# Splitting batch 0's state operands in high and low parts from the fifth step on

## The chip, the cores and the metric

One core of a Trainium2 chip runs the whole program. The metric is the device time of one execution in microseconds (us); of several runs the median is given. [...]

## What is computed

Three stages follow each other. `x` has 8 batches of 8 heads, 512 rows and 64 columns, and `state` has 32 rows for each head.

```
scores  = x @ state.T / 8          a  = softmax(scores)     xread = a  @ state
scores2 = state @ x.T / 8          a2 = softmax(scores2)    sread = a2 @ x
X   = concat(xread, sread) over rows, heads side by side     (4352 x 512)
X1  = (silu(X @ w_gate) * (X @ w_val)) @ w_out               (512 -> 1536 -> 512)
out = (h * sigmoid(1.702 h)) @ w2_out,  h = X1 @ w2_in       (512 -> 2048 -> 512)
```

All is fp32. The change is in the second line block, in `X @ w_gate` and `X @ w_val` of batch 0.

## The kernel before

**Weights through the state.** `xread` is never formed. Since `X @ w = a @ (state @ w)`, the kernel multiplies the states with the weights first. One such product, `sw[b, u, g]`, belongs to a batch b, a pair u of steps and a group g of four heads: 128 rows (four heads by 32 states) by 512 columns. `quad_job` (L615) makes them for four batches at a time: two matmuls (L628) of 64 contraction rows, two copies out of PSUM into a tile `qs` (L634 on ScalarE, L635 on VectorE), and a store of the rows of the other batches to DRAM through ScalarE's DMA queue (`move`, L651). Batch 0's own rows go from `qs` straight into the operand tile by SyncE's queue (L647), for u from `OWN` = 2 on. For u below 2, `state_weights` makes batch 0's operand directly.

**Two kinds of product.** Matmuls on plain fp32 operands (`mm_whole`, L336) stand in the trace as two MATMUL records each. The other way splits each operand in a high part that is rounded to the type fp32r and the low part that is left over, and takes three passes: high by high, low by high, high by low (`mm_rows`, L329 to L331). `mm_state` (L710) makes the products of a step with the states' weights: batch 0 takes the plain way, all others the split one.

**Steps.** A block of 512 rows (a batch) takes F1 = 12 steps f of 128 columns. A step has a gate product, work of its places 0, a value product, work of place 1, the output product of the step before (12 matmuls of three passes, L951 to L953), and work of place 2. Steps 2u and 2u + 1 use `sw[b, u, g]`. ScalarE takes Silu of the gate product (L976), VectorE multiplies (L991), then the result is split for the output product: high part on ScalarE (L796), low part on VectorE, or on GpSimd in batch 0 (L797).

**What else batch 0 carries.** While batch 0's steps run (about 25 to 160 us), all weights arrive and are put together from two halves of their bits, `whole_slot`: L202 and L203 on ScalarE, L211 and L212 on VectorE, L215 on GpSimd; the weights of `w_out` are split too (L249, L250). The attention of batch 1 is done beside it (table `BLOCK0`): scores (copied by L461), maximum (L488, L492), exponentials (L502, L507, each with a load of ScalarE's function table before and after), sums, transposes (L539).

**Order.** The program is recorded in the order in which it is written, each engine keeps its own order of instructions, and so do the DMA queues. `plan_weights` puts work at (step, place), here by `job_places` for `quad_job`. For later batches it puts `fetch` (a DMA from DRAM into a tile `xf` of which there are two, on ScalarE's queue, L660) one step ahead of `cut_fetched` (L666 on ScalarE, L667 on GpSimd), which splits that tile into an operand `xo`. Batch 1's fetches for u = 0 stand at step 9 of batch 0.

Of the kernel before, what the change touches and what calls it, by code (L numbers as in the profile page):

```python
# [8 lines left out]
F32 = mybir.dt.float32  # L9
# [3 lines left out]
ALU = mybir.AluOpType  # L13
# [60 lines left out]
def kernel(  # L74
# [25 lines left out]
    NS = state.shape[2]  # L100
    DM = H * D
    FF1 = w_gate.shape[1]
    FF2 = w2_in.shape[1]
    P = 128
    KD = DM // P
    F1 = FF1 // P
    U1 = F1 // 2
# [7 lines left out]
    v, a, pe, pool_e, sy = nc.vector, nc.scalar, nc.tensor, nc.gpsimd, nc.sync  # L115
# [4 lines left out]
    work = ctx.enter_context(tc.tile_pool(name="work", bufs=2))  # L120
    xp = ctx.enter_context(tc.tile_pool(name="xop", bufs=1))
# [13 lines left out]
    def f32(t):  # L135
        return t.bitcast(F32)
# [147 lines left out]
    def need_whole(key):  # L284
        while pos["done"] <= where[key]:
            before = pos["done"], pos["begun"]
            whole_slot()
            assert before != (pos["done"], pos["begun"]), key
# [37 lines left out]
    def mm_rows(ps, pairs):  # L326

        for k, (wh, wl, xh, xl) in enumerate(pairs):
            pe.matmul(ps, wh, xh, start=k == 0, stop=False)  # L329
            pe.matmul(ps, wl, xh, start=False, stop=False)  # L330
            pe.matmul(ps, wh, xl, start=False, stop=k == len(pairs) - 1)  # L331

    def mm_whole(ps, pairs):

        for k, (w, x_) in enumerate(pairs):
            pe.matmul(ps, w, x_, start=k == 0, stop=k == len(pairs) - 1)  # L336
# [14 lines left out]
    def at():  # L351
        if extra:
            extra.append(extra.pop(0))
            if extra[0] != "at":
                return psa.tile([P, 512], F32, name="at", tag=extra[0])
        return pst.tile([P, 512], F32, name="at", tag="at")
# [246 lines left out]
    sw = {}  # L603
# [13 lines left out]
    OWN = 2  # L617

    def quad_job(qd, u, k, late=False):


        if qd == 0:
            need_whole(("gv", u, k))
        w = whole[u * KD + k]
        ps = [at(), at()]
        for hl in range(2):
            r = slice(hl * 64, hl * 64 + 64)
            pe.matmul(ps[hl], quad_t[qd][r, k], w[r], start=True, stop=True)  # L628
        pos["jobs"] += 1
        if qd == 0 and not late or pos["jobs"] % 3 == 0:  # L630
            t = ap.tile([P, 2, DM], F32, name="qs", tag="qs", bufs=2)
        else:
            t = work.tile([P, 2, DM], F32, name="qs", tag="raw", bufs=RAWS)
        a.copy(t[:, 0], ps[0])  # L634
        v.tensor_copy(t[:, 1], ps[1])  # L635
        g, q = divmod(k, 2)
        skip = NS * (1 - qd)
        if q == 0:
            quads[qd, u, g] = dp.tile([4 * (P - skip), DM], F32, name=f"sw{qd}_{u}_{g}")
        rows = quads[qd, u, g].rearrange("(q h p) m -> q p h m", q=2, h=2)  # L640
        moved[qd].append((rows[q], t[skip:]))
        if qd == 0 and u >= OWN:
            if q == 0:
                sw[0, u, g] = x_tiles(xp, u % 2 * 2 + g, DM)
            for hl in range(2):
                r = slice(q * 64 + hl * NS, q * 64 + hl * NS + NS)
                sy.dma_start(f32(sw[0, u, g][0][r]), t[:NS, hl])  # L647

    def move():
        for to, t in moved.pop(0):  # L650
# [3 lines left out]
    fetched = {}  # L654
# [7 lines left out]
    def cut_fetched(b, u, g, home=None):  # L662
        t = fetched.pop((b, u, g))
        pl, tag = home or (xp, f"x{u % 2 * 2 + g}")
        x_ = pl.tile([P, 2, DM], F32R, name="xo", tag=tag)
        a.copy(x_[:, 0], t)  # L666
        pool_e.tensor_tensor(x_[:, 1], t, f32(x_[:, 0]), op=ALU.subtract)  # L667
        sw[b, u, g] = x_[:, 0], x_[:, 1]

    def job_places(b):  # L670

        if b == 0:
            own = [-2, 0, 1, 2]
            first = [(n, 0, k) for k, n in enumerate((0, 1, 2, 3))]
            last = [(n, 1, k) for k, n in enumerate((28, 30, 32, 34))]
            return [(n, 0, u, k) for n, u, k in first + last] + [
                (6 * (u - 1) + own[k], 0, u, k) for u in range(OWN, U1) for k in range(KD)
            ]
        if b < 4:
            return [(n, 1, *divmod(8 * (b - 1) + j, KD)) for j, n in enumerate((3, 6, 12, 15, 18, 24, 30, 33))]  # L680
        return []

    def plan_weights(plan, i):


        b = order1[i]
        nb = order1[i + 1] if i + 1 < NB1 else None
        if nb == B:
            nb = None

        def put(f, place, fn, *args):
            plan.setdefault((f, place), []).append(lambda: fn(*args))

        for n, qd, u, k in job_places(b):
            put(n // 3, n % 3, quad_job, qd, u, k, n >= 3 * F1 - 6)
        for g in range(2):
            if 0 < b < B:
                put(b == 1, g, cut_fetched, b, 1, g)
                if b == 1:
                    put(0, g + 1, fetch, b, 1, g)  # L700
                for u in range(2, U1):
                    put(2 * u - 3, g + 1, fetch, b, u, g)
                    put(2 * u - 2, g + 1, cut_fetched, b, u, g)
            if nb is not None:
                put(9, g, fetch, nb, 0, g)
                put(10, g, cut_fetched, nb, 0, g, (ae, f"a{g}") if b == B else None)
                if nb > 1:
                    put(11, g, fetch, nb, 1, g)

    def mm_state(ps, b, f, t):  # L710

        c = slice(t * 2 * P + f % 2 * P, t * 2 * P + f % 2 * P + P)
        pairs = []
        if b == 0:
            mm_whole(ps, [(f32(sw[b, f // 2, g][0])[:, c], f32(groups[b, g].a[:, 0])) for g in range(2)])
            return
        for g in range(2):
            wh, wl = sw[b, f // 2, g]
            at_ = groups[b, g].a
            pairs.append((wh[:, c], wl[:, c], at_[:, 0], at_[:, 1]))  # L720
        mm_rows(ps, pairs)
# [6 lines left out]
    groups = {}  # L728
# [70 lines left out]
    def x_tiles(pl, k, N):  # L799
        t = pl.tile([P, 2, S], F32R, name="xo", tag=f"x{k}")  # L800
        return t[:, 0, :N], t[:, 1, :N]
# [98 lines left out]
    for i, blk in enumerate(order1):  # L900
# [5 lines left out]
        if blk + 1 < B:  # L906
            plan_batch(plan, blk + 1)
        plan_weights(plan, i)
        if i == NB1 - 3:
            plan.setdefault((F1 - 2, 2), []).append(load_tail)  # L910
# [51 lines left out]
        def product(ps, f, t):  # L962
            if not tail:
                mm_state(ps, blk, f, t)
                return
            c = slice(t * 2 * P + f % 2 * P, t * 2 * P + f % 2 * P + P)
            w = [units["gv", f // 2, k] for k in range(KD)]
            mm_rows(ps[:, :N], [(w[k][:, 0, c], w[k][:, 1, c], *xop[k]) for k in range(KD)])
# [362 lines left out]
```

## Time and profile before

| what | value |
|---|---|
| median of 3 runs | 1504.39 us (1501.16 to 1505.3) |
| the profiled execution's own time | 1508.42 us |
| its span, first to last instruction | 1506.6 us |
| TensorE (PE) busy | 1475.1 us, 98% |
| VectorE (DVE) busy | 913.0 us, 61% |
| ScalarE (ACT) busy | 685.0 us, 45% |
| GpSimd (POOL) busy | 394.8 us, 26% |
| mean granted clock of TensorE | 0.992 |

The shares are means over the whole program. Batch 0 is about a tenth of it and has its own limits, so it has to be read by its stretches of time. Times in rows are us from the start of the span; where a row groups several records, the second number is the time from the first's start to the last's end. A matmul's own length includes what overlaps with the next one, so the cost of a matmul is the distance from one start to the next.

### The profile page before, as it was taken

The page shows a single profiled execution, that of the slowest core. Times are in us where ns is not written, and L with a number is a line of the kernel's source. Part 1 is how long each engine was busy: PE and PEld are TensorE (multiplying, and loading weights), DVE is VectorE, ACT ScalarE, POOL GpSimd, SP SyncE. Part 2 cuts the span into 40 slices and gives each one's busy share as a digit, 9 for nine tenths or more (in the row PEclk, how much of TensorE's full clock was granted, in tenths as well). Part 3 has the DMA queues.
Part 4 walks back from the last instruction along what each step waited for, and adds up shares of the span by engine and source line. Part 5 has one row for each costly group of instructions (what it writes and reads, how often), then busy time and mean ns, then how long its engine had stood idle before and what let it go on. Part 6 is the DMA issues. An engine that isn't in the chain of part 4 may idle for free.

```text
span 1506.6 us, 21223 instructions
## 1 busy us (share of the span) xinstructions
PE 1475.1 (98%) x7688; PEld 1197.5 (79%) x7688; DVE 913.0 (61%) x1600; ACT 685.0 (45%) x1247; POOL 394.8 (26%) x325
## 2 busy tenths in 40 slices
PE   7989999999999999999999999999999999999998
PEld 3445677777787777889788889999999999999997
DVE  6885565656679887953334335665655666656554
ACT  6766454545567666644454333233332333333222
POOL 2665322222234544556655421000000000000000
PEclk8999999999999999999999999999999999999999
DMA  7974333333455655422766656565565656564653
GB/s 212 293 239 144 123 109 116 114 110 109 134 183 168 193 178 179 138 85 82 234 233 248 232 184 209 187 222 171 193 215 185 221 180 238 168 238 159 214 183 130
DMA packets 138480, 269.30 MB, mean 179 GB/s; under 512 B 46728, under 2 KB 57992, under 8 KB 138376
## 3 DMA queue, kind: packets, MB, share of 16 engines
q1 hardware_dynamic: 114680, 223.64, 45.4%
q10 hardware_dynamic: 23696, 44.31, 8.9%
q8 instruction: 61, 1.00, 0.3%
q14 instruction: 43, 0.35, 0.1%
HBM read 202.11 MB, written 63.70 MB: 176 GB/s over the span
## 4 chain that ended last, share of the span: by engine, by line
PE 56%; DMA 7%; DVE 3%; ACT 2%; issue 2%; POOL 1%; ACTq 0%; SPq 0%; POOLq 0%; DVEq 0%
PE acc L339 8%; PE acc L340 8%; PE acc L341 8%; DMA xf<-sw 5%; PE gv L1232 4%; PE gv L1231 4%; PE gv L1230 4%; PE at L1230 3%; PE at L1231 3%; PE at L1232 3%; PE gv L329 2%; PE gv L330 1%; PE gv L331 1%; PE acc L953 1%; PE gv L322 1%
## 5 line engine op out<-in xcount | busy, mean ns | idle before, releaser
L797 DVE TENSOR_TENSOR h<-sg,h 128x512 fp32r<-128x512 f32 (+1 forms) x240 | 191.6, 798 | 136.2 <-ACT h L796 134.3
L796 ACT CAST h<-sg 128x512 fp32r<-128x512 f32 (+1 forms) x251 | 149.8, 597 | 183.8 <-DVE sg L991 80.8
L339 PE MATMUL acc<-wo,h 128*128 128x512 f32 x512 | 200.6, 392 | 0.0
L340 PE MATMUL acc<-wo,h 128*128 128x512 f32 x512 | 200.6, 392 | 0.0
L341 PE MATMUL acc<-wo,h 128*128 128x512 f32 x512 | 199.2, 389 | 0.0
L667 POOL TENSOR_TENSOR xo<-xf,xo 128x512 fp32r<-128x512 f32 x84 | 112.4, 1341 | 240.5 <-ACT xo L666 234.2
L1254 ACT ACTIVATE sg<-wt 128x512 f32<-128x512 f32 x56 | 35.4, 632 | 299.9 <-DVE wt L1252 299.9
L951 PE MATMUL acc<-h,wu 128*128 128x512 f32 (+1 forms) x428 | 166.6, 389 | 0.0
L953 PE MATMUL acc<-h,wu 128*128 128x512 f32 (+1 forms) x428 | 163.9, 383 | 1.9 <-DVE h L797 1.9
L952 PE MATMUL acc<-h,wu 128*128 128x512 f32 (+1 forms) x428 | 163.6, 382 | 0.0
L329 PE MATMUL gv<-a,xo 128*128 128x512 f32 x336 | 139.6, 415 | 3.8 <-ACT sg L976 3.5
L330 PE MATMUL gv<-a,xo 128*128 128x512 f32 x336 | 134.2, 399 | 0.0
L331 PE MATMUL gv<-a,xo 128*128 128x512 f32 x336 | 133.6, 398 | 0.0
L991 DVE TENSOR_TENSOR sg<-gv,sg 128x512 f32<-128x512 f32 (+1 forms) x107 | 70.5, 659 | 89.5 <-PE gv L331 31.6
L341 PEld LDWEIGHTS acc<-wo,h 128*128 128x128 f32 x512 | 96.2, 188 | 20.9
L339 PEld LDWEIGHTS acc<-wo,h 128*128 128x128 f32 x512 | 96.6, 189 | 17.1
L340 PEld LDWEIGHTS acc<-wo,h 128*128 128x128 f32 x512 | 96.6, 189 | 15.8
L1252 DVE TENSOR_TENSOR wt<-wt,gv 128x256 f32<-128x256 f32 x56 | 23.6, 421 | 136.8 <-PE gv L1232 136.8
L951 PEld LDWEIGHTS acc<-h,wu 128*128 128x128 f32 x428 | 81.1, 189 | 24.0 <-issue 7.6
L953 PEld LDWEIGHTS acc<-h,wu 128*128 128x128 f32 x428 | 81.1, 189 | 19.9 <-DVE h L797 3.8
L1232 PE MATMUL gv<-xo,wu 128*128 128x256 f32 x336 | 95.4, 284 | 0.0
L1231 PE MATMUL gv<-xo,wu 128*128 128x256 f32 x336 | 95.1, 283 | 0.0
(178 smaller groups left out, 3407.2 us busy)
## 6 DMA issues: line engine op xcount, KB each, us to landing
wo<-w2b SPq DMA_DIRECT2D x128, 512.0 KB
wc<-w2c SPq DMA_DIRECT2D x84, 512.0 KB
xf<-sw ACTq DMA_DIRECT2D x84, 256.0 KB
raw<-in_moe_w_out_dram SPq DMA_DIRECT2D x28, 512.0 KB
sw<-qs ACTq DMA_DIRECT2D x24, 512.0 KB
sw<-qs ACTq DMA_DIRECT2D x24, 384.0 KB
xn<-in_x_dram SPq DMA_DIRECT2D x16, 512.0 KB
y<-ev SPq DMA_DIRECT2D x16, 512.0 KB
```

Of the source, the lines that this page charges most:

```text
L329: pe.matmul(ps, wh, xh, start=k == 0, stop=False)
L330: pe.matmul(ps, wl, xh, start=False, stop=False)
L339: pe.matmul(ps, lh, rh, start=first, stop=False)
L340: pe.matmul(ps, lh, rl, start=False, stop=False)
L341: pe.matmul(ps, ll, rh, start=False, stop=last)
L796: a.copy(h_, src)
L797: eng.tensor_tensor(l_, src, f32(h_), op=ALU.subtract)
L951: pe.matmul(ps, w[:, 0, c], h[:, 0, :N], start=f == 0, stop=False)
L952: pe.matmul(ps, w[:, 1, c], h[:, 0, :N], start=False, stop=False)
L953: pe.matmul(ps, w[:, 0, c], h[:, 1, :N], start=False, stop=f == F1 - 1)
L1231: pe.matmul(ps, w[:, 1, c], x_[:, 0, kt], start=False, stop=False)
L1232: pe.matmul(ps, w[:, 0, c], x_[:, 1, kt], start=False, stop=kt == 1)
```

## The change

From step 4 (u = 2) on, batch 0's products with the states' weights take the split way. For this its own rows no longer go into the operand tile but into a tile `xf`, and `cut_fetched` splits that at step 2u - 1, place g. The other operand, the attention weights `a` of batch 0 (one tile for each group), is split once, after the last plain product: `cut_own` copies it on VectorE, ScalarE writes the rounded high part into a new tile, and VectorE subtracts. It stands at step 3, place 1 for the first group and place 2 for the second.

```diff
         if qd == 0 and u >= OWN:
             if q == 0:
-                sw[0, u, g] = x_tiles(xp, u % 2 * 2 + g, DM)
+                fetched[0, u, g] = work.tile([P, DM], F32, name="xf", tag="xf", bufs=2)
             for hl in range(2):
                 r = slice(q * 64 + hl * NS, q * 64 + hl * NS + NS)
-                sy.dma_start(f32(sw[0, u, g][0][r]), t[:NS, hl])
+                sy.dma_start(fetched[0, u, g][r], t[:NS, hl])
...
+    def cut_own(g):
+        t = work.tile([P, DM], F32, name="wt", tag="wt", bufs=3)
+        v.tensor_copy(t, f32(groups[0, g].a[:, 0]))
+        groups[0, g].a = a_ = groups[0, g].a_tile()
+        a.copy(a_[:, 0], t)
+        v.tensor_tensor(a_[:, 1], t, f32(a_[:, 0]), op=ALU.subtract)
...
         for g in range(2):
+            if b == 0:
+                put(3, 1 + g, cut_own, g)
+                for u in range(OWN, U1):
+                    put(2 * u - 1, g, cut_fetched, b, u, g)
             if 0 < b < B:
...
         pairs = []
-        if b == 0:
+        if b == 0 and f // 2 < OWN:
             mm_whole(ps, [(f32(sw[b, f // 2, g][0])[:, c], f32(groups[b, g].a[:, 0])) for g in range(2)])
```

In the changed kernel the lines behind `cut_own` stand 11 lower: L796 becomes L807, L976 L987, L991 L1002.

On VectorE at steps 3 and 4 of batch 0, before the change, from one copy of `quad_job` to the next:

```order
L635 COPY qs<-at 128x512
L211 TENSOR_SCALAR wf<-wf 128x512
L212 SCALAR_TENSOR_TENSOR wf<-raw,wf 128x512
L499 TENSOR_TENSOR sp<-sp,sq 128x512
L211 TENSOR_SCALAR wf<-wf 128x512
L212 SCALAR_TENSOR_TENSOR wf<-raw,wf 128x512
L211 TENSOR_SCALAR wt<-wt 128x512
L212 SCALAR_TENSOR_TENSOR wt<-raw,wt 128x512
L635 COPY qs<-at 128x512
```

The same stretch with the change:

```order
L635 COPY qs<-at 128x512
L672 COPY wt<-a 128x512
L675 TENSOR_TENSOR a<-wt,a 128x512
L211 TENSOR_SCALAR wf<-wf 128x512
L212 SCALAR_TENSOR_TENSOR wf<-raw,wf 128x512
L499 TENSOR_TENSOR sp<-sp,sq 128x512
L672 COPY wt<-a 128x512
L675 TENSOR_TENSOR a<-wt,a 128x512
L211 TENSOR_SCALAR wf<-wf 128x512
L212 SCALAR_TENSOR_TENSOR wf<-raw,wf 128x512
L211 TENSOR_SCALAR wt<-wt 128x512
L212 SCALAR_TENSOR_TENSOR wt<-raw,wt 128x512
```

The two copies and the two subtractions of `cut_own` stand ahead of the weight work and of the next copy of `quad_job`; each subtraction reads what ScalarE writes between it and the copy.

On ScalarE at step 3, with the change, from the copy of `quad_job` to the second part of `cut_own`:

```order
L634 COPY qs<-at 128x512
L674 CAST a<-wt 128x512
L666 CAST xo<-xf 128x512
L807 CAST h<-sg 128x512
L249 CAST wu<-wt 128x512
L202 ACTIVATE wf<-raw 128x512
L203 ACTIVATE raw<-raw 128x512
L651 DMA sw_3_0_702<-qs 96x2x512
L502 ACT_TABLE_LOAD
L502 ACTIVATE sp<-sp 128x512
L507 ACTIVATE e_742,sm<-ST,sm 128x512
L674 CAST a<-wt 128x512
```

Before, L634 was followed at once by the cast of h, and neither L674 nor L666 stood here; the cast of the second group now comes behind the exponentials of batch 1 and their table load.

On ScalarE at step 9, with the change, with what each instruction waits for:

```order
L461 COPY ST<-at 128x512 [waits PE_49]
L666 CAST xo<-xf 128x512
L660 DMA xf<-sw_0_0_373 128x1x512 [waits Pool_49]
L249 CAST wu<-wt 128x512
L634 COPY qs<-at 128x512 [waits DMAHW6_49,DMAHW7_49,DMAHW0_49,PE_49]
L666 CAST xo<-xf 128x512 [waits DMAHW2_49,DMAHW1_49]
L660 DMA xf<-sw_0_1_440 128x1x512 [waits Pool_49]
L807 CAST h<-sg 128x512 [waits DVE_49]
```

Before, the two L666 were not there and the two L660 waited for nothing. Each L660 now waits until GpSimd has subtracted from the `xf` tile that it refills (L667), and ScalarE's later instructions stand behind it.

## Rows read from the trace of the kernel before

**Rows 1.** Busy time by stretch of batch 0: steps 3/4, 5, 6 to 8, 9 to 11.
```profile
core 0: us, PE busy (x) PEld busy (x) DVE busy (x) ACT busy (x) POOL busy (x), PEclk, DMA share, GB/s
71.00:91.00 20.00, 16.59 (x44) 8.51 (x44) 18.29 (x25) 13.97 (x23) 13.15 (x11) 0.83 0.79 248
91.00:105.00 14.00, 13.45 (x45) 7.17 (x44) 11.88 (x19) 10.08 (x18) 8.39 (x7) 1.00 0.82 249
105.00:131.00 26.00, 26.00 (x91) 12.83 (x90) 13.54 (x19) 14.42 (x27) 15.80 (x12) 1.00 0.64 193
131.00:160.00 29.00, 28.32 (x91) 14.66 (x92) 15.63 (x29) 14.99 (x25) 11.88 (x9) 1.00 0.41 113
```

**Rows 2.** Timeline, TensorE, step 4: start, length, engine, line, operation, idle before.
```profile
73.77 1.88 PE L336 MATMUL gv<-a,xo 128*128 128x512 f32 x4
75.58 1.13 PE L628 MATMUL at<-wf,qt 64*128 64x512 f32 x4
...
82.03 2.96 PE L628 MATMUL at<-wf,qt 64*128 64x512 f32 x4 [3.41 <-DVE qs L635]
84.92 0.80 PE L951 MATMUL acc<-h,wu 128*128 128x512 f32 x1
...
90.30 1.13 PE L628 MATMUL at<-wf,qt 64*128 64x512 f32 x4
91.36 1.98 PE L336 MATMUL gv<-a,xo 128*128 128x512 f32 x4
```

**Rows 3.** Stretch within step 4: PE busy, granted clock, DMA share, GB/s.
```profile
85.00:90.00 5.00, 5.00 (x12) 0.50 0.65 201
```

**Rows 4.** Timeline, TensorE, first split product of batch 1 (six passes from 160.42).
```profile
160.42 0.40 PE L329 MATMUL gv<-a,xo 128*128 128x512 f32 x1
...
161.83 0.39 PE L951 MATMUL acc<-h,wu 128*128 128x512 f32 x1
```

**Rows 5.** Timeline, VectorE, steps 3 and 4.
```profile
74.30 0.69 DVE L635 COPY qs<-at 128x512 f32<-128x512 f32 x1
...
76.41 0.68 DVE L499 TENSOR_TENSOR sp<-sp,sq 128x512 f32<-128x512 f32 x1
77.01 1.52 DVE L211 TENSOR_SCALAR wf<-wf 128x512 uint32<-128x512 uint32 x1
...
79.17 0.42 DVE L211 TENSOR_SCALAR wt<-wt 128x512 uint32<-128x512 uint32 x1
...
81.21 0.68 DVE L635 COPY qs<-at 128x512 f32<-128x512 f32 x1
...
87.91 0.68 DVE L635 COPY qs<-at 128x512 f32<-128x512 f32 x1
```

**Rows 6.** Timeline, ScalarE, step 3 into step 4.
```profile
72.19 0.62 ACT L796 CAST h<-sg 128x512 fp32r<-128x512 f32 x1 [0.59 <-DVE sg L991]
...
75.42 1.28 ACT L502 ACT_TABLE_LOAD   x1 [0.63 <-ACT raw L203]
...
78.27 0.19 ACT L507 ACTIVATION_READ_ACCUMULATOR e<-ST,sm 128x1 f32 x1
```

**Rows 7.** Lines L667 and L666, later batches: duration ns min/median/max.
```profile
L667 POOL TENSOR_TENSOR xo<-xf,xo x84: 1263/1294/1785, 145.9 to 765.4; 128x512 fp32r<-128x512 f32 x84
...
L666 ACT CAST xo<-xf x84: 603/621/638, 145.2 to 764.6; 128x512 fp32r<-128x512 f32 x84
```

**Rows 8.** Timeline, TensorE, step 6, its only wait between 91 and 150 us.
```profile
104.53 1.09 PE L628 MATMUL at<-wf,qt 64*128 64x512 f32 x2 [0.55 <-DVE srd L574]
```

**Rows 9.** Timelines, steps 9 and 10: ScalarE, VectorE, TensorE.
```profile
134.57 0.58 ACT L461 COPY ST<-at 128x512 f32<-128x512 f32 x1 [1.12 <-PE at L336]
...
137.92 0.62 ACT L796 CAST h<-sg 128x512 fp32r<-128x512 f32 x1
...
142.30 0.69 DVE L510 TENSOR_REDUCE sq<-sp 128x16 f32<-128x512 f32 x1 [0.72 <-ACT sp L502]
...
144.12 0.69 DVE L635 COPY qs<-at 128x512 f32<-128x512 f32 x1
...
144.96 0.63 PE L539 MATMUL at<-ident,e 128*128 128x128 f32 x4
```

## The prediction

> **What bounds the kernel now.** I first read the busy time by stretch. TensorE is busy 98% of the span, but in batch 0 that is not so everywhere: at steps 3 and 4 it worked 16.59 of 20 us while VectorE worked 18.29, and at step 5 VectorE worked 11.88 of 14 us; from step 6 on VectorE is half idle and TensorE almost never [rows 1]. So there are two regimes: up to about 105 us VectorE's queue decides, behind that TensorE does.
>
> The timeline shows what this means. TensorE reaches a pair of `quad_job` matmuls in step 4 and waits 3.41 us for VectorE's copy of `quad_job` [rows 2], which starts at 81.21 [rows 5]. [...] Then VectorE's rows: one weight operation takes 0.42 us alone and 1.52 us at 77.01 [rows 5], where it stands beside work of GpSimd. Last I read what ScalarE does at steps 3 and 9, since the change puts new work ahead of things that others wait for.
>
> **The change part by part.**
>
> *Products.* A plain product of two groups takes 75.58 - 73.77 = 1.81 us [rows 2], a split one 161.83 - 160.42 = 1.41 us [rows 4]. Sixteen products (steps 4 to 11, two each) by 0.40 give 6.4 us. That is the whole gain, and it counts only where TensorE is the limit.
>
> *Step 4, where `cut_own` is waited for.* VectorE's copy at 74.30 ends its work for step 3's `quad_job`, 0.6 us later the new copy can start. Nothing in the trace is this copy; the nearest is the uncontended weight operation on the same shape, 0.42 us [rows 5]. So the copy ends at 75.35, ScalarE's cast (0.6, as L666 [rows 7]) at 75.95, the subtraction (0.65, as the VectorE subtraction at 76.41 [rows 5]) at 76.6. Meanwhile ScalarE has stood still: before, its cast of h began at 72.19 [rows 6], now it comes behind the first `cut_own` cast and an L666, at 76.5. From that cast to the end of the exponentials ScalarE took 78.46 - 72.19 = 6.27 us, 1.3 of it idle [rows 6]. So the second cast of `cut_own` starts between 81.5 and 82.8, and the second subtraction ends at about 83.1. TensorE needs it for the last pass of step 4's gate product, which ended at 75.58 before [rows 2]. TensorE thus loses nearly 8 us here, against 3.41 in the wait that it had.
>
> The old wait does not simply go into the new one. Behind the second subtraction VectorE still has four weight operations to do before the next copy of `quad_job`: 81.21 - 77.01 = 4.2 us with their collisions, 2.2 without. If the two new GpSimd subtractions (1.29 each [rows 7]) collide with VectorE's work at step 3 as well, everything there is up to 2.2 later. That copy starts between 85.3 and 89.4 instead of at 81.21. The copy after it came 6.70 us behind [rows 5], and TensorE began step 5 at 91.36, so 3.45 us after that [rows 2]; at full clock TensorE needs only 1.2 us there. Step 5 then begins between 93.2 and 97.3 if VectorE leads, and at 91.0 if VectorE meets no collision at all and the clock stays full. The cost is between -0.4 and +5.9 us, and up to +8 if all of the output product runs at the lower clock again. I take **+3.5**: VectorE led before and gets more work, and the lower clock mostly falls into time in which TensorE waits for VectorE anyway.
>
> *Steps 5 to the first product of 6.* Three products get 0.40 faster each, but TensorE waited here for VectorE already, at 104.53 [rows 8], and VectorE is 85% busy [rows 1]. Two new GpSimd subtractions come in. If VectorE had room, -1.2; if each holds VectorE up for its whole length, 2 x 1.29 = +2.6. I take **+1**. [...]
>
> *From the second product of step 6 to step 8.* TensorE is the limit (26.00 of 26 us busy [rows 1]), VectorE and ScalarE are half idle and the casts and subtractions for u = 4 and 5 (0.62 and 1.29 us each [rows 7]) lie beside TensorE. Without that cover they would cost 1.9 us each. Five products: **-2.0**, 0 at worst.
>
> *Steps 9 and 10.* Both fetches of batch 1 now wait for GpSimd on ScalarE's queue, and behind them stand the cast of h and batch 1's exponentials. Walked through from the copy at 134.57 [rows 9]: L666 ends at 135.7, the subtraction at 137.0, then the fetch, L249, the copy of `quad_job` and the second L666 to 138.7. GpSimd does its weight subtraction and then the second cut to 140.2, the second fetch goes, and the cast of h starts near 140.6 instead of 137.92. All that follows on ScalarE is 2.7 us late, 2.3 with the gate product's 0.40 taken off. VectorE's sums wait for the exponentials (142.30), the copy of `quad_job` stands behind them (144.12) and TensorE's transposes (144.96) behind that copy [rows 9]. TensorE, which would have been 1.6 us early, has to wait nearly 4 us there. Bounds: -1.6 if ScalarE had that time to spare, +2.1 as walked, and 2.6 more if the clock drops behind this wait as it did behind that of 3.41 us (half of 5.38). I take **+2.1**. On SyncE's queue the stores to `xf` wait for a cut two steps back, which by then is done; I cost that at nothing.
>
> *Step 11.* Two products, **-0.8**; no new work stands there.
>
> Sum: 3.5 + 1 - 2.0 + 2.1 - 0.8 = **+3.8 us**. The profiled execution took 1508.42 us, so the same one would take 1512.2; the median of the runs shown, 1504.39, lies 4.0 lower, which gives **1508.2**. A measurement of this kernel can tell about 0.3%, 4.5 us, from no change.
>
> **The rivals.**
>
> *Every collision takes place (slower).* The new GpSimd subtractions of steps 3 and 5 each hold VectorE up for their whole length: 5.9 + 2.6 - 2.0 + 2.1 - 0.8 = +7.8, 1512.2 us. For it: VectorE works 18.29 of 20 us there, and a collision such as that at 77.01 costs it 1.1 us [rows 1, 5]. Against it: not all of its work is of the kind that gets longer; its copies out of PSUM took 0.68 or 0.69 us at 74.30, 81.21 and 87.91 alike [rows 5]. It decides from steps 4 to 6 costing 5.2 us together. [...] Chance 0.29.
>
> *The clock drops in step 10 too (slower).* The new wait before the transposes is about as long as the one after which the clock fell: 3.8 + 2.6 = +6.4, 1510.8 us. For it: the one example in step 4. Against it: shorter work follows. Chance 0.14.
>
> *The stalls cover each other (faster).* Step 4's old wait and its lower clock, 3.41 and 2.7 us, vanish into the new wait, and ScalarE's delay at step 9 is absorbed: -0.4 - 1.2 - 2.0 - 1.6 - 0.8 = -6.0, 1498.4 us. For it: TensorE would do less work in a kernel it bounds by 98%. Against it: at step 3 VectorE reaches `cut_own` only at 74.9. Chance 0.10.
>
> **How the numbers follow.** The forecast, within 0.3% on the slow side, has 0.47; the two slower rivals 0.43 together, the faster one 0.10. The predicted time is 1508.2 us. The range goes from 1501, which leaves the faster rival out, to 1514, above the worst collisions with some of the clock.
>
> **What would show it.** In the new profile, step 4's gate product should end 9 to 12 us after it could have begun (1.8 before), its last wait on the `cut_own` subtraction; the next copy of `quad_job` on VectorE should start 4 to 8 us later than before; split products should stand 1.41 us apart; and TensorE should wait 3 to 4 us before the transposes of step 10. I am wrong if step 4's product waits less than 4 us, if TensorE does not wait in step 10, or if the time from 105 to 131 us shrinks by less than 1.5 us.

## The result, and the profile after

The changed kernel takes **1516.99 us** (median of 4 runs, 1516.39 to 1517.93), the kernel before beside it 1503.95: ratio 1.0089, 95% interval 1.0075 to 1.0103. That is 13.0 us slower, 3.0 us beyond the end of the range (1514) and 8.8 beyond the forecast. The profiled execution took 1517.93 us with a span of 1516.0.

The same four stretches as in [rows 1], in the changed kernel:

```profile
core 0: us, PE busy (x) PEld busy (x) DVE busy (x) ACT busy (x) POOL busy (x), PEclk, DMA share, GB/s
71.00:91.00 20.00, 11.85 (x33) 6.01 (x32) 17.91 (x23) 14.26 (x24) 12.93 (x11) 0.66 0.62 198
91.00:105.00 14.00, 14.00 (x58) 9.22 (x56) 13.67 (x16) 10.33 (x19) 10.57 (x8) 1.00 0.76 245
105.00:131.00 26.00, 22.12 (x78) 12.67 (x76) 15.28 (x25) 13.35 (x24) 17.93 (x14) 0.87 0.60 185
131.00:160.00 29.00, 24.34 (x90) 15.00 (x88) 15.73 (x24) 17.08 (x29) 15.89 (x13) 0.95 0.38 107
```

Between 91 and 105 us VectorE is now busy 13.67 of 14 us. TensorE, which never rested from 105 to 131 us before, does so for 3.9 us there, and for 4.7 in the last stretch; the granted clock of TensorE (PEclk, a share of the full one) is under 1.00 in three stretches (0.66, 0.87, 0.95), where before it was in one (0.83).

TensorE's timeline, which answers to [rows 2, 4, 8] and the end of [rows 9]:

```profile
74.53 0.50 PE L329 MATMUL gv<-a,xo 128*128 128x512 f32 x1 [2.09 <-ACT a L674]
...
82.11 0.80 PE L329 MATMUL gv<-a,xo 128*128 128x512 f32 x1 [6.07 <-ACT a L674]
...
83.69 2.08 PE L628 MATMUL at<-wf,qt 64*128 64x512 f32 x4
...
94.47 0.50 PE L329 MATMUL gv<-a,xo 128*128 128x512 f32 x1
...
110.25 2.04 PE L628 MATMUL at<-wf,qt 64*128 64x512 f32 x2 [3.87 <-DVE srd L574]
112.23 0.79 PE L329 MATMUL gv<-a,xo 128*128 128x512 f32 x1
...
138.32 0.49 PE L329 MATMUL gv<-a,xo 128*128 128x512 f32 x1
...
149.15 0.50 PE L330 MATMUL gv<-a,xo 128*128 128x512 f32 x1 [1.12 <-POOL xo L667]
...
156.07 0.63 PE L539 MATMUL at<-ident,e 128*128 128x128 f32 x4 [3.54 <-ACT sg L987]
```

Four of these waits are new: two in step 4's gate product (each for a cast of `cut_own`), and two in step 10, for a low part and before the transposes. The one in step 6 was 0.55 us before. The three places by stretch, with the granted clock of TensorE near the end of each row (columns as in the first view above):

```profile
75.00:89.00 14.00, 7.93 (x18) 3.71 (x18) 12.75 (x14) 11.73 (x19) 9.65 (x7) 0.51 0.49 156
...
109.00:116.00 7.00, 5.75 (x10) 2.83 (x12) 3.57 (x8) 1.74 (x3) 3.19 (x3) 0.51 0.48 155
157.00:160.00 3.00, 3.00 (x8) 2.32 (x7) 0.81 (x2) 2.56 (x6) 2.92 (x3) 0.50 0.81 208
```

VectorE's timeline in steps 3 to 6, beside [rows 5]:

```profile
73.41 0.42 DVE L672 COPY wt<-a 128x512 f32<-128x512 f32 x1
74.50 0.69 DVE L675 TENSOR_TENSOR a<-wt,a 128x512 fp32r<-128x512 f32 x1 [0.68 <-ACT a L674]
75.11 1.52 DVE L211 TENSOR_SCALAR wf<-wf 128x512 uint32<-128x512 uint32 x1
...
78.23 1.74 DVE L499 TENSOR_TENSOR sp<-sp,sq 128x512 f32<-128x512 f32 x1
79.90 1.50 DVE L672 COPY wt<-a 128x512 f32<-128x512 f32 x1
82.09 0.69 DVE L675 TENSOR_TENSOR a<-wt,a 128x512 fp32r<-128x512 f32 x1 [0.69 <-ACT a L674]
...
85.84 0.69 DVE L635 COPY qs<-at 128x512 f32<-128x512 f32 x1
...
94.58 0.69 DVE L635 COPY qs<-at 128x512 f32<-128x512 f32 x1 [0.15 <-PE at L628]
...
108.94 1.17 DVE L574 TENSOR_SCALAR srd<-at,sm 32x64 f32<-32x64 f32 x4 [0.47 <-DVE sm L571]
```

The same copy, L672, takes 0.42 us at 73.41, where GpSimd is idle (72.48 to 75.07), and 1.50 at 79.90, beside GpSimd's L215 (79.39 to 81.12). ScalarE's timeline in step 9, beside [rows 9] (ACTq is its sequencer, which issues the DMA):

```profile
142.22 0.63 ACT L666 CAST xo<-xf 128x512 fp32r<-128x512 f32 x1
144.23 1.10 ACTq L660 DMA_DIRECT2D xf<-sw  x1
145.37 0.62 ACT L249 CAST wu<-wt 128x512 fp32r<-128x512 f32 x1 [2.52 <-issue]
...
149.13 0.53 ACTq L660 DMA_DIRECT2D xf<-sw  x1
149.71 0.62 ACT L807 CAST h<-sg 128x512 fp32r<-128x512 f32 x1 [2.71 <-POOL xo L667]
```

### The profile page after: what moved, and what is told of

It is laid out like the page before. It is cut to its first block, busy times and chain, and to the rows that moved or that the text cites. A ratio compares the mean times of both kernels' runs of the same rounds, so it can differ in the third digit from the quotient of the medians.

```text
span 1516.0 us, 21305 instructions
## 1 busy us (share of the span) xinstructions
PE 1472.5 (97%) x7720; PEld 1202.4 (79%) x7720; DVE 928.4 (61%) x1604; ACT 689.6 (45%) x1257; POOL 407.6 (27%) x333
## 4 chain that ended last, share of the span: by engine, by line
PE 54%; DMA 4%; issue 3%; DVE 2%; POOL 2%; ACT 2%; ACTq 0%; SPq 0%; POOLq 0%; DVEq 0%
PE acc L339 8%; PE acc L340 8%; PE acc L341 8%; PE gv L1243 4%; PE gv L1242 4%; PE gv L1241 3%; PE at L1241 3%; PE at L1242 3%; PE at L1243 3%; DMA xf<-sw 2%; PE gv L322 1%; PE gv L324 1%; PE gv L323 1%; PE acc L964 1%; PE gv L329 1%
## 5 line engine op out<-in xcount | busy, mean ns | idle before, releaser
L807 ACT CAST h<-sg 128x512 fp32r<-128x512 f32 (+1 forms) x251 | 149.7, 597 | 190.0 <-DVE sg L1002 84.0
L667 POOL TENSOR_TENSOR xo<-xf,xo 128x512 fp32r<-128x512 f32 x92 | 123.1, 1341 | 241.5 <-ACT xo L666 236.0
L329 PE MATMUL gv<-a,xo 128*128 128x512 f32 x368 | 154.7, 420 | 11.5 <-ACT a L674 8.2
L330 PE MATMUL gv<-a,xo 128*128 128x512 f32 x368 | 147.7, 401 | 1.2 <-POOL xo L667 1.1
L331 PE MATMUL gv<-a,xo 128*128 128x512 f32 x368 | 147.0, 400 | 0.0
L1002 DVE TENSOR_TENSOR sg<-gv,sg 128x512 f32<-128x512 f32 (+1 forms) x107 | 70.4, 658 | 85.1 <-PE gv L331 35.9
L329 PEld LDWEIGHTS gv<-a,xo 128*128 128x128 f32 x368 | 69.7, 189 | 57.1 <-issue 26.0
L1243 PE MATMUL gv<-xo,wu 128*128 128x256 f32 x336 | 95.5, 284 | 0.0
```

Source lines behind the costliest of these rows:

```text
L807: a.copy(h_, src)
L1243: pe.matmul(ps, w[:, 0, c], x_[:, 1, kt], start=False, stop=kt == 1)
```

## The experiments

All runs change the changed kernel unless they say otherwise. "Now" is the median, the ratio is that to the kernel before beside it (medians 1502.0 to 1503.0 us). Theory A: three places cost, each by itself. Theory B: VectorE's queue as a whole is the limit, and a wait taken away comes back in the next place. Theories C, D and E came up on the way and are told where they do. The kernel before measured 1503.95 us beside the changed kernel, up to 1.9 us more than beside the others, so a difference between the changed kernel and a later run is safer read from the ratios.

To compare places I use the same marks on TensorE in each profile: the starts of the value product of step 3, the gate product of step 5, the value product of step 6, and the gate products of steps 9, 11 and of batch 1 (68.04, 91.36, 105.56, 130.83, 149.34 and 160.42 us in the kernel before; 66.54, 94.47, 112.23, 138.32, 162.01 and 172.43 in the changed one). Lengths in us, each from one profiled execution:

| kernel | step 3/4 | 5 to 6 | 6 to 8 | 9, 10 | 11 | sum |
|---|---|---|---|---|---|---|
| before | 23.32 | 14.20 | 25.27 | 18.51 | 11.08 | 92.38 |
| changed | 27.93 | 17.76 | 26.09 | 23.69 | 10.42 | 105.89 |
| `own_early` | 26.97 | 16.56 | 25.73 | 23.71 | 12.02 | 104.99 |
| `late_fetch` | 27.80 | 17.76 | 25.97 | 18.88 | 10.64 | 101.05 |
| `no_sub` | 25.99 | 16.05 | 25.52 | 18.79 | 10.44 | 96.79 |
| `work_only` | 28.05 | 17.23 | 26.45 | 25.11 | 11.06 | 107.90 |
| `own_home` | 26.16 | 16.92 | 27.00 | 18.86 | 10.83 | 99.77 |
| `own_home_no_sub` | 23.26 | 14.67 | 25.14 | 18.09 | 10.83 | 91.99 |
| `own_home_dve` | 24.28 | 16.03 | 25.18 | 18.68 | 11.36 | 95.53 |
| `before_order` | 23.33 | 12.57 | 25.28 | 18.32 | 11.16 | 90.66 |
| `no_sub_order` | 22.17 | 12.44 | 24.26 | 17.64 | 11.72 | 88.23 |

### Batch 1's fetches behind the exponentials: `late_fetch`

```diff
-                put(9, g, fetch, nb, 0, g)
+                put(9, g if b else 2, fetch, nb, 0, g)
```

> Changed kernel with batch 1's two fetches for u = 0 moved from step 9, places 0 and 1, to step 9, place 2, behind the exponentials on ScalarE. Theory A: TensorE's wait before the transposes of step 10 (3.5 us) and the one for GpSimd before it (1.1 us) go, and with them the lower clock behind it: 1511 to 1512. Theory B: the transposes still wait for VectorE, 1516 to 1517.

Now 1511.72 us, ratio 1.0065 (1.0053 to 1.0077): 5.3 us less by the medians, 3.6 by the ratios, 4.8 in the two profiles. That fits A. Steps 9 and 10 go from 23.69 to 18.88 us and nothing comes back behind them. What is left there, from the waits of its TensorE:

```profile
PE at L539 <- DVE qs L635: 1.6, 1, 1.6
```

Counted from the start of step 9, TensorE arrives 1.28 us earlier than in the kernel before (at 151.67 less 138.82, against 144.96 less 130.83), which is the gain of the products, and VectorE's copy starts 0.38 us later (152.49 less 138.82, against 144.12 less 130.83).

### `cut_own`'s copies earlier: `own_early`

```diff
+    def own_copy(g):
+        own_full[g] = t = work.tile([P, DM], F32, name="wt", tag="wt", bufs=3)
+        v.tensor_copy(t, f32(groups[0, g].a[:, 0]))
...
-                put(3, 1 + g, cut_own, g)
+                put(2, 1 + g, own_copy, g)
+                put(3, 1, cut_own, g)
```

> Changed kernel with the copies of cut_own moved to step 2, both casts and both subtractions together at step 3, place 1, ahead of the exponentials. Theory A (three places cost separately: cut_own behind the exponentials at step 4, GpSimd's subtractions against VectorE at step 5, the fetches that wait on ScalarE at step 9): TensorE's wait in step 4's gate product falls from 6.1 to under 2 us, and the time from 1517.0 to about 1513. Theory B (VectorE's queue is the limit as a whole, and a wait that goes in one place comes back in the next): the wait moves to the next copy of quad_job, and the time stays at 1516 to 1517.

Now 1514.86 us, ratio 1.0088 (1.0073 to 1.0103). The 8.2 us of waits for `cut_own` fall to 2.4 (now for its subtractions), but TensorE stands again at the next copy of `quad_job`:

```profile
85.56 3.25 PE L628 MATMUL at<-wf,qt 64*128 64x512 f32 x4 [4.40 <-DVE qs L635]
```

Step 3/4 becomes 1.0 us shorter, not 4, and the ratio is that of the changed kernel (1.0089). Here B is right about the place: VectorE works without a gap from 74.79 to 85.51 us, and its next result is what TensorE then waits for.

### GpSimd's subtractions left out: `no_sub`

```diff
         a.copy(x_[:, 0], t)
+        if b == 0:
+            sw[b, u, g] = x_[:, 0], x_[:, 0]
+            return
```

> Changed kernel without GpSimd's eight subtractions for batch 0: the high part of the states' weights stands for the low part too, so that the passes are as many (the low part of that operand is left out of the result). Theory A: steps 5 to 8 take back 3.6 + 2.8 us, the fetches at step 9 wait for nothing (about 5 us), and step 4 gets about 1.5 us shorter: near 1504. Theory B, with VectorE's own added work (2.2 us) and cut_own's chain as the whole cost: 1513 or more.

Now 1508.63 us, ratio 1.0044 (1.0032 to 1.0055): 8.4 us less by the medians, 6.8 by the ratios, between both theories. It contains what `late_fetch` gave, since a fetch waits for no subtraction any more; 3.1 us are its own (1511.72 to 1508.63).

### The split from step 8 on only: `from_u4`, `from_u4_home`

`from_u4` splits only u = 4 and 5, with `cut_own` at step 7 and the later fetches.

```diff
-                put(3, 1 + g, cut_own, g)
-                for u in range(OWN, U1):
+                put(7, 1 + g, cut_own, g)
+                for u in range(CUT, U1):
```

> Products split only from step 8 on (u = 4 and 5), cut_own at step 7, batch 1's fetches for u = 0 at step 9, place 2. Theory A: cut_own and four cuts lie where VectorE and ScalarE are half idle, eight products save 0.4 us each and nothing is waited for: about 1501, 3 us under the kernel before. Theory B: cut_own's chain and the cuts stall TensorE wherever they stand: 1506 or more.

Now 1505.89 us, ratio 1.0021 (1.0010 to 1.0032): no gain, though eight products at the prediction's price of 0.40 us each would give 3.2 us. TensorE waited 1.7 and 1.0 us for `cut_own`. `from_u4_home` takes that away: the plain `a` of both groups lies in a tile of batch 1 that is unused until step 10, so `cut_own` needs neither a copy nor the last plain product, and stands at step 6.

> Split products only from step 8 on (u = 4 and 5, eight products), with batch 0's plain a of both groups in a tile that batch 1 uses only from step 10 on, and both parts of cut_own at place 2 of step 6, where VectorE waits for TensorE. from_u4, where cut_own came behind the last plain product of step 7, measured 1505.9 us and waited 1.7 + 1.0 us for it. Theory A: these 2.7 us go, 1503.2 us, and with the products' 8 x 0.40 all of it realised not below 1500.7 us. Theory B (the added work of ScalarE and VectorE costs as much as the products give, wherever it stands): 1504 us or more. Theory C: as A, 1501 to 1503 us.

Now 1502.82 us, ratio 1.0001 (0.9992 to 1.0009). As A and C said for the wait, but the products' gain still does not show. In its profile it is used up in three places: step 8 takes 10.41 us (120.25 to 130.66) against 9.87 before, TensorE waits 1.66 us before the transposes of step 10, and in step 11 the clock falls to half behind a wait that the kernel before has too (156.49, there with the clock at 1.00):

```profile
156.42 1.12 PE L636 MATMUL at<-wf,qt 64*128 64x512 f32 x2 [0.68 <-ACT qs L642]
157.48 0.70 PE L975 MATMUL acc<-h,wu 128*128 128x512 f32 x1
```

The output product behind it takes 4.45 us (157.48 to 161.93) instead of 2.87 (157.55 to 160.42).

### `cut_own` in another tile: `own_home`, `own_home_no_sub`, `own_home_dve`

The in-place split of `a` was why `cut_own` had to copy and to wait. In these kernels the plain `a` lies in tiles that batch 1's `a` takes from step 5 on, and both splits stand at step 2:

```diff
-            self.a = self.a_tile()
+            self.a = ao.tile([P, 2, S], F32R, name="a", tag=f"a{self.g}") if self.b == 0 else self.a_tile()
...
-        t = work.tile([P, DM], F32, name="wt", tag="wt", bufs=3)
-        v.tensor_copy(t, f32(groups[0, g].a[:, 0]))
-        groups[0, g].a = a_ = groups[0, g].a_tile()
+        t = f32(groups[0, g].a[:, 0])
+        own[g] = a_ = groups[0, g].a_tile()
...
-                put(3, 1 + g, cut_own, g)
+                plan.setdefault((2, 2), []).insert(g, lambda g=g: cut_own(g))
```

The fetches are as in `late_fetch`. Theory C is that each new wait is paid twice, in itself and in the lower clock behind it.

> The changed kernel with batch 1's two fetches at place 2 of step 9 (as in late_fetch, measured 1511.7 us), and with batch 0's plain a kept in the tile that batch 1's a uses later, so that cut_own needs no copy and no finished plain product: both casts and both VectorE subtractions stand at place 2 of step 2, where VectorE and ScalarE were idle. Theory A (each place has its own cost; the +4.7 us of step 4 are the wait for cut_own): step 4 has only the wait for the copy of quad_job that the kernel before had, about 1507 us. Theory C (each new wait is paid twice, in itself and in the lower clock behind it): step 4 gives back its lower clock as well, 1504 us or less. Theory B (VectorE's queue as a whole is the limit, what goes in one place comes back in the next): 1509 us or more.

Now 1509.70 us, ratio 1.0047 (1.0034 to 1.0059): 2.0 us less than `late_fetch` (2.7 by the ratios), B's figure. Step 3/4 still takes 2.8 us more than in the kernel before, with nothing of `cut_own` in it. With the edit of `no_sub` on top, `own_home_no_sub`:

> As own_home, but GpSimd's subtraction for batch 0's operands is left out (the high part stands for the low one, so batch 0's products are not those of the reference). What is left of the change are the split products, ScalarE's casts and the two early subtractions of cut_own. Theory A: the subtractions cost what no_sub gained beyond late_fetch, 1511.7 - 1508.6 = 3.1 us, so 3 us less than own_home, about 1504 us. Theory C: step 6 has no wait over 2 us and no lower clock, and the sixteen products give 4 to 6 us: 1499 us or less. Theory B: as own_home within 1.5 us.

Now 1503.20 us, ratio 1.0004 (0.9994 to 1.0013): 6.5 us less than `own_home`, so theory A's figure for the time, at twice its price for the subtractions. Steps 3/4 and 5 to 6 are back at 23.26 and 14.67 us. VectorE's timeline shows why, first `own_home` from one copy of `quad_job` to the next:

```profile
74.11 0.69 DVE L635 COPY qs<-at 128x512 f32<-128x512 f32 x1
...
75.34 1.65 DVE L212 SCALAR_TENSOR_TENSOR wf<-raw,wf 128x512 uint32<-128x512 uint32 x1
76.92 1.78 DVE L499 TENSOR_TENSOR sp<-sp,sq 128x512 f32<-128x512 f32 x1
78.62 1.50 DVE L211 TENSOR_SCALAR wf<-wf 128x512 uint32<-128x512 uint32 x1
...
82.81 0.68 DVE L635 COPY qs<-at 128x512 f32<-128x512 f32 x1
```

and the same in `own_home_no_sub`:

```profile
74.18 0.69 DVE L635 COPY qs<-at 128x512 f32<-128x512 f32 x1
...
75.70 0.69 DVE L212 SCALAR_TENSOR_TENSOR wf<-raw,wf 128x512 uint32<-128x512 uint32 x1
76.31 0.69 DVE L499 TENSOR_TENSOR sp<-sp,sq 128x512 f32<-128x512 f32 x1
76.91 1.52 DVE L211 TENSOR_SCALAR wf<-wf 128x512 uint32<-128x512 uint32 x1
...
81.12 0.68 DVE L635 COPY qs<-at 128x512 f32<-128x512 f32 x1
```

The two copies stand 8.70 us apart and 6.94 us apart, with the same instructions in the same order between them. GpSimd's timeline of `own_home` beside it:

```profile
73.76 1.27 POOL L667 TENSOR_TENSOR xo<-xf,xo 128x512 fp32r<-128x512 f32 x1
74.99 1.46 POOL L809 TENSOR_TENSOR h<-sg,h 128x512 fp32r<-128x512 f32 x1
76.41 1.74 POOL L250 TENSOR_TENSOR wu<-wt,wu 128x512 fp32r<-128x512 f32 x1
78.11 1.73 POOL L215 TENSOR_TENSOR wf<-wf,raw 128x512 uint32<-128x512 uint32 x1
```

The subtraction (L667) is over before the first long VectorE instruction starts at 75.34. What the three stand beside is GpSimd's work behind it, L809, L250 and L215, which it has pushed back and which runs without a gap; without it GpSimd is idle from 75.38 to 76.47, and only one of the three is long. (A fourth long one, L212 just ahead of the last copy, is in both: 1.67 and 1.66 us.) `own_home_dve` has batch 0's subtractions on VectorE; theory D is that GpSimd's own queue being late is what costs.

```diff
-        pool_e.tensor_tensor(x_[:, 1], t, f32(x_[:, 0]), op=ALU.subtract)
+        (pool_e if b else v).tensor_tensor(x_[:, 1], t, f32(x_[:, 0]), op=ALU.subtract)
```

> own_home (measured 1509.7 us, with the subtractions left out 1503.2 us) with the subtractions of batch 0's operands on VectorE instead of GpSimd. Theory A (the 6.5 us between those two are VectorE's instructions getting longer while GpSimd subtracts): four of the eight subtractions lie where VectorE decides, at about 0.69 us each without making others longer, so about 1506 us, and the copies of quad_job of step 4 stand about 8.3 us apart (8.70 in own_home, 6.94 without subtractions). Theory D (GpSimd's own queue is late, and what it feeds with it): no subtraction on GpSimd, 1503 to 1504.5 us. Theory B (VectorE's queue as a whole, any added work goes through it in full): 1508.5 us or more.

Now 1506.53 us, ratio 1.0024 (1.0014 to 1.0033), A's figure for the time. VectorE does the subtraction itself and is still faster from copy to copy, 7.54 us (A had 8.3):

```profile
75.00 0.69 DVE L635 COPY qs<-at 128x512 f32<-128x512 f32 x1
75.61 1.13 DVE L667 TENSOR_TENSOR xo<-xf,xo 128x512 fp32r<-128x512 f32 x1
...
82.54 0.68 DVE L635 COPY qs<-at 128x512 f32<-128x512 f32 x1
```

### The work without the gain: `work_only`

```diff
-        if b == 0 and f // 2 < OWN:
+        if b == 0:
```

> The changed kernel with all its casts, subtractions and copies, but batch 0's products stay plain, on the high parts alone (so they are not those of the reference): the work without the gain. Theory A: the products' gain counts from the second product of step 6 on, eleven products by 0.40 us, so 4.4 us more than the changed kernel's 1517.0: 1521 us, and step 4 waits only for the last cast, not for the last subtraction. Theory C or B, in which the gain is swallowed by waits and the lower clock behind them: 1517 to 1519 us.

Now 1516.81 us, ratio 1.0095 (1.0081 to 1.0109): the same as the changed kernel within the intervals. The shorter products are worth nothing that can be told from the noise there (2.0 us by the two profiles, 105.89 against 107.90; 0.9 by the ratios); A's 4.4 us lies outside.

### Where the gain goes: the order of two pieces

Two pieces of batch 1's attention stand in VectorE's queue ahead of what TensorE waits for: the scaling of step 6 (`state_sum`, L570 to L574) and the sums of step 10 (L510 to L515). The edit moves the first one pair of weight operations earlier and the second behind the copy of `quad_job`:

```diff
-    (5, 2): "G0.state_read",
-    (6, 0): "G0.state_sum",
+    (5, 2): "G0.state_read G0.state_sum",
...
-    (10, 0): "G1.sum_n G1.over_sum:v",
-    (10, 1): "G1.turn_e G1.back",
+    (10, 1): "G1.sum_n G1.over_sum:v G1.turn_e G1.back",
```

On `own_home`, as `own_home_order`:

> own_home with two pieces of batch 1's attention in another place of VectorE's order: the scaling that TensorE waits for in step 6 (state_sum) stands one pair of weight operations earlier, and the sums of step 10 stand behind the copy of quad_job that TensorE's transposes wait for. Theory A (each wait is a matter of its own place): the wait of 3.6 us in step 6 falls to about 0.5, the lower clock behind it (1.2 us) goes with it, the 1.6 us of step 10 go: 1509.7 - 3.1 - 1.2 - 1.6 = 1503.8 us. Theory B (a queue that is full hands the wait on to the next copy): 1508 us or more.

Now 1506.34 us, ratio 1.0022 (1.0011 to 1.0033): 3.4 of the 5.9 us. The wait of step 6 is down to 0.19 us, that before the transposes of step 10 is gone, and the clock is 1.00 from 105 to 131 us, but TensorE now waits 0.93 us in step 8 for a low part from GpSimd, and 1.05 and 1.43 us for ScalarE's copies at the end of step 10 and in step 11. On `from_u4_home`, as `from_u4_order`:

> from_u4_home (split products from step 8 on, measured 1502.8 us against 1503.0 for the kernel before) with the same two pieces in the same new places. Theory A: the 1.7 us wait before the transposes of step 10 and the 0.6 us of step 6 go, 1500.5 us. Theory B: 1502.5 us or more.

Now 1504.40 us, ratio 1.0006 (0.9994 to 1.0018): nothing gained, as B said. On the kernel before, `before_order`, and a second time, `before_order_again`:

> The kernel before, unchanged but for the same two pieces in the same new places, so that what the order alone is worth can be taken off from_u4_order. It waits 0.55 us in step 6 and not at all before the transposes of step 10. Theory A: 0.5 us less than the kernel before, 1502.5 us. Theory B: no change.

> before_order once more, beside the other two on the same chip: it measured 1501.8 us, 0.12% less than the kernel before with an interval that nearly reaches no change. Expected 0.998 to 0.9995 of the kernel before; if the first result was chance, 1.000.

Now 1501.83 us, ratio 0.9988 (0.9978 to 0.9998), and 1500.85 us, 0.9996 (0.9985 to 1.0007). Both lie below the kernel before, by 0.04 to 0.12%; the second interval takes in no change. On `own_home_no_sub`, as `no_sub_order`, where theory E is that the gain is lost wherever other engines pace batch 0:

> own_home_no_sub (measured 1503.2 us; batch 0's low parts replaced by the high ones, no subtraction on GpSimd for them) with the two pieces of batch 1's attention in the new places of own_home_order. It has nearly none of the change's added work in VectorE's crowded stretch, and no wait in step 6 behind which the clock could fall. Theory C (the products' gain is real, but it goes into the wait of step 6, the lower clock behind that, and the wait of step 10): 1.9 + 1.2 + 0.9 us come free, 1499.2 us, granted clock 1.00 from 105 to 131 us. Theory E (the gain is lost wherever VectorE or ScalarE paces batch 0, and TensorE only arrives earlier at its next wait): 1501.5 us or more.

Now 1500.32 us, ratio 0.9985 (0.9974 to 0.9996), 2.9 us less than `own_home_no_sub`, between C and E. GpSimd's low parts are left out of it, so its result is not that of the reference. The stretch from 105 to 131 us, first of `own_home_no_sub`:

```profile
105.00:131.00 26.00, 26.00 (x102) 16.16 (x102) 14.08 (x20) 14.77 (x27) 15.02 (x12) 0.93 0.60 182
```

and of `no_sub_order`:

```profile
105.00:131.00 26.00, 26.00 (x106) 16.36 (x104) 13.81 (x19) 16.51 (x31) 17.02 (x13) 1.00 0.65 200
```

TensorE is busy all the time in both; the clock is what differs, 0.93 against 1.00. Beside `before_order` the sum of the places is 88.23 against 90.66 us: in the two profiles 2.4 of the 6.4 us arrive, with none of GpSimd's subtractions for batch 0 in the way and the clock at 1.00 in that stretch. The medians differ by less, 0.5 us from `before_order_again` and 1.5 from `before_order`, and the intervals of the ratios overlap, so this gain is not clear of the noise. Last, every repair that keeps the whole computation, `own_home_dve_order` (`own_home_dve` with the same order):

> The whole change with every repair at once: plain a in the other tile and split early, batch 1's fetches later, batch 0's subtractions on VectorE, the two pieces of attention in their new places. own_home_dve measured 1506.5 us. If the savings add as in own_home_order (3.4 us): 1503.1 us, the same as the kernel before. Theory C: 1501 us or less, and faster than before_order, which has the order alone. Theory E: 1503 us or more.

Now 1503.63 us, ratio 1.0009 (1.0000 to 1.0018): E's figure, and the sum that the text works out. It is not faster than the kernel before. In its profile, too, the clock fell in step 11 behind a wait of 0.67 us, and the output product there took 4.45 us. `before_order`, without the change, has the lowest medians of the kernels that compute everything, and those are hardly below the kernel before.

## Why the prediction was wrong

The sign of the sum and the places of the cost held. The sizes did not, and the gain was priced by a condition that the change itself removed: the sum was +3.8 us and the places give +13.5 in the two profiles (+13.0 by the medians). By the last of its own signs the prediction was wrong: the stretch from step 6 to step 8 was to shrink by at least 1.5 us, and it grew by 0.8.

| term | predicted | found |
|---|---|---|
| step 4, `cut_own` | +3.5 (-0.4 to +5.9) | +4.6 |
| step 5 to first product of 6 | +1 (-1.2 to +2.6) | +3.6 |
| second product of 6 to step 8 | -2.0 (0 at worst) | +0.8 |
| steps 9 and 10 | +2.1 (up to +4.7) | +5.2 |
| step 11 | -0.8 | -0.7 |

**Step 4** came as walked through: the gate product ended 11.2 us after it could have begun (83.69 less 74.53 - 2.09 = 72.44; 9 to 12 predicted). TensorE entered it 1.3 us earlier than in the profile before (73.77), so VectorE's next copy of `quad_job` is to be taken relative to that: 13.40 us behind (85.84 - 72.44) against 7.44 (81.21 - 73.77) before, 6.0 us later (4 to 8 predicted). One sign was off: the product's last wait is for the cast (82.11, its releaser L674), and not for the subtraction, which ended at 82.78, before the pass that reads it (83.13). What the text took as one cost is two, which do not add: without the subtractions (`no_sub`) step 3/4 costs 2.7 us more than before, without the waits for `cut_own` (`own_home`) 2.8, with both 4.6, with neither (`own_home_no_sub`) nothing.

**Steps 5 and 6** are the first step that failed. The text took +1 between "if VectorE had room, -1.2" and "if each holds VectorE up for its whole length, 2 x 1.29 = +2.6". In size it is the second. From the start of step 5 to the end of L574 the changed kernel takes 15.64 us (94.47 to 110.11), the kernel before 13.02 (91.36 to 104.38, just ahead of the matmul of [rows 8]): 2.62 us more.

```profile
103.22 1.16 DVE L574 TENSOR_SCALAR srd<-at,sm 32x64 f32<-32x64 f32 x4
```

That this is so near to 2 x 1.29 is in part luck: in `no_sub`, which has neither subtraction, the same way still takes 13.93 us (94.16 to 108.09), so the two account for 1.71 of the 2.62 us. The same comparison of `own_home` and `own_home_no_sub` gives 1.68 (15.18 and 13.50 us). The other 0.91 us stays open. Another 0.95 us is the clock, for which the text had nothing here: the matmul behind the wait takes 1.98 us to the next product instead of 1.03 (110.25 to 112.23 at 0.51; 104.53 to 105.56 before, at 1.00). The rival "every collision takes place" had the size of VectorE's part right here; that a GpSimd instruction holds VectorE up for its whole length was an assumption, which no run shows. What the rows show is which instructions got longer beside GpSimd's work: L499 and L212, which take two SBUF tiles, went from 0.69 us (`own_home_no_sub`) to 1.78 and 1.65 us (`own_home`), and two that take one tile, L211 in `own_home` and L672 in the changed kernel, from 0.42 to 1.50 us. The copies L635 out of PSUM take 0.68 or 0.69 us in every row above, also at 74.11 in `own_home`, beside GpSimd's L667 (73.76 to 75.03). Why the ones got longer and the others did not was not shown.

**Steps 6 to 8** failed in its condition, which the text named and then did not carry through: "TensorE is the limit" was read from a stretch that began behind a wait of 0.55 us. Behind 3.87 us the clock fell to 0.51, and the way from the value product of 6 to the gate product of 7 took 8.31 us (112.23 to 120.54) against 6.98. Step 7's two products did give 0.71 us, step 9's 0.66, so 0.33 to 0.36 a product, not 0.40. So the sign that split products stand 1.41 us apart was not met: in step 7 it is 1.51 (120.54 to 122.05), as the first pass takes 0.33 us to the next (120.54 to 120.87) and the others 0.23 or 0.24. The price of [rows 4] was read directly behind an output product. Step 8 gave nothing: 10.07 us to the next gate product against 9.87 before and 9.30 in `no_sub`, so there the low parts from GpSimd cost what the products gave.

**Steps 9 and 10** were walked through rightly but for a length of time that was left out: the DMA issues. The walk had the cast of h 9.8 us after the start of the step (140.6 - 130.83); it came 11.4 behind (149.71 - 138.32). Most of the difference, 1.6 us, is the issue of the first L660, 1.10 us, for which the walk had counted nothing and behind which L249 stands (2.52 us of waiting in its row); another 0.43 is the second subtraction, 1.72 us long (from 147.38, behind L250) instead of 1.29. The issue is there in the kernel before as well, but half of it is hidden there behind L461 [rows 9], and L249 waits 0.57 us:

```profile
134.58 1.10 ACTq L660 DMA_DIRECT2D xf<-sw  x1
135.72 0.62 ACT L249 CAST wu<-wt 128x512 fp32r<-128x512 f32 x1 [0.57 <-issue]
```

The row of the transposes names ScalarE's Silu (L987, ended at 156.01) as what they waited for last; VectorE's copy, which the walk had as the last, ended at 155.93, so the two came almost together. The rest of the term is the rival "the clock drops in step 10 too": 4.9 us instead of 3.3 from the transposes to step 11 (156.07 to 160.96; 144.96 to 148.28), at a clock of 0.50. The 2.6 us that the text gave the lower clock are about half of the output product of [rows 2], 5.38 us from 84.92 to 90.30 at the 0.50 of [rows 3]; at 1.00 one takes 2.87 us (157.55 to 160.42 in the kernel before). That rival was given 0.14, and its mechanism took place together with that of the other slower rival; the text priced them one at a time and put the end of the range at 1514, with "some of the clock" on the worst collisions. The two together, from the text's own terms, are 5.9 + 2.6 - 2.0 + 4.7 - 0.8 = +10.4, 1514.8 us.

**The gain** of 6.4 us was the largest error in kind. At 0.33 to 0.36 a product in place, sixteen products are 5.3 to 5.8 us. That does not arrive where VectorE or ScalarE pace the step (steps 4 to 6, and step 10 with its wait of 1.6 us in `late_fetch`), and where TensorE is the limit the lower clock or GpSimd's low parts take it. `work_only` shows that it is worth nothing clear of the noise in the changed kernel; in `no_sub_order` 2.4 us by the profiles, 0.5 to 1.5 by the medians, are left when most else is out of the way. How the remaining 3 us or so divide among the pacing engines was not taken apart.

## What to carry to other kernels

Work that is added in a stretch where another engine already sets the pace is to be priced by what it does to that engine's queue (here 1.8 us for one subtraction at step 3, 1.7 for two at step 5), and the time saved on the waiting engine at nothing; a stretch counts as bound by an engine only as long as the waits ahead of it stay as they are (here one went from 0.55 to 3.87 us, and the clock behind it from 1.00 to 0.51). Where two stalls can happen, price them together as well as apart. When an instruction is put ahead of a queue's DMA, count the issue of the DMA itself (1.10 us for the first L660), and look whether an in-place update is what forces the copy and the wait: another tile that is free for those steps took both away.

## What was not expected of the hardware

Moving the eight subtractions from GpSimd (1.27 to 1.75 us each in the changed kernel) to the busier VectorE (19.63 of 20 us against GpSimd's 15.25 from 71 to 91 us in `own_home`) made the kernel 3.2 us faster (1509.70 to 1506.53).

TensorE's granted clock fell to 0.51 (109 to 116 us) behind a wait of 3.87 us in the changed kernel, and in `own_home_no_sub` to a mean of 0.63 (104 to 108 us) behind one of 1.95 us; in `late_fetch` it stayed at 1.00 (154 to 160 us) behind the 1.65 us before the transposes. The length of the wait alone does not tell, though. In `own_home_dve` the passes behind a longer one start 0.23 or 0.24 us apart (78.86 to 79.80), as they do at 1.00 in step 7 of the changed kernel, where at 0.51 they start 0.42 or 0.43 apart (112.82 to 114.53):

```profile
76.80 0.50 PE L330 MATMUL gv<-a,xo 128*128 128x512 f32 x1 [2.22 <-DVE xo L667]
```

And behind the wait of 0.67 or 0.68 us in step 11, which the kernel before and the others have in the same place, the clock fell in three kernels, `own_early`, `from_u4_home` and `own_home_dve_order`, and in no other; each time the output product took 4.45 or 4.46 us instead of 2.84 to 2.88. So a wait can cost more than its own length, and which one does could not be read from its length here. Each of these kernels has one profiled execution only.
